# A new hand-written order for one segment of a memory recurrence, with filler copies, head sums and fold read at places of their own

## The chip, the cores and the metric

The kernel runs on one core of one Trainium2 chip. The metric is device time in microseconds of one execution; the profile is of one execution of the same program, taken by the hardware profiler, and its times are us from the first instruction.

## What is computed

Two attention blocks over the same 2048 tokens of width 576 are mixed by a gate. Block B is ordinary attention with 32 heads of width 18. Block A is a recurrence over 64 segments of 32 tokens: each segment sees 8 memory tokens and its own 32, and its first 8 outputs are the memory of the next.

```python
def _A_ref(x, mem0, Wq, Wk, Wv, Wo, seg_len):
    ...
    for s in range(n_seg):
        h = jnp.concatenate([mem, xs], axis=1)           # 8 + 32 tokens
        q, k, v = (einsum('btd,dhe->bhte', h, W) for W in (Wq, Wk, Wv))   # 32 heads of 128
        p = _softmax(where(mask, einsum('bhqe,bhke->bhqk', q, k) * scale, -1e9))
        o = einsum('bhte,hed->btd', einsum('bhqk,bhke->bhqe', p, v), Wo)
        mem = o[:, :M, :]
        outs.append(o[:, M:, :])
def _B_ref(x, wqkv, wo): ...                             # softmax attention, 32 heads of 18, no mask
return g * a + (1 - g) * b                               # g = sigmoid((x * gate_w).sum(-1))
```

## The kernel before, in words

**The stages.** A first part turns x, projects B's q, k and v and loads A's weights. Then come the 64 segments of A, one after the other; steps of B's attention are put between the steps of each segment. A last part finishes B, projects it out and mixes. The change lies in the segments and in two helpers that feed them.

**B's steps.** `b_steps` is a generator. Its first half, written `B` in the order, puts four score matmuls into `sb` (four PSUM banks, one buffer) and then the four value matmuls of the step before into `ob` (one bank, `values`, L239). Its second half, `E`, is one exp on ScalarE from `sb` to `etb` (L291). So the next `sb` has to wait for this exp, and the values come one step later. Every 16 steps a block of 512 queries is done: `ob` holds the sums and the weighted values of the 18-wide heads, and `divisions` (L178) puts six parts into the list `late`: two `turn_in` (a VectorE transpose that reads `ob`, L187), and then divide and turn_out twice. The next block can write `ob` only after both turn_in. `late_part` (L173) emits one part; `/` in the order calls it. Before the first value matmul of a new block all pending turn_in are emitted (L243).

**A segment.** The 32 kept tokens of `ht` (8 memory, 24 new; the last 8 tokens of each segment are projected ahead of time) go through these steps, with b = 0, 1 for two halves of the heads:

- Qb, Kb, Vb: projections into `pvv` (L672), 20 matmuls of 512 columns, four at a time on 32 columns of the array; cQb, cKb, cVb: copies to SBUF on VectorE (L684); vb: four DMAs on SP's queue that lay V out by heads in `v_sb` (L689).
- tqb, tkb: four transposes each into one PSUM tile `pt` (L699); pqb, pkb: the copies out of it (L707).
- Sb: scores into `psh` (L717); xb: exp on ScalarE (L728); nb: the causal minimum (L732); pb: sums by a matmul with `bsel` into `pss` (L739); lb, rb: log and exp(-log) on ScalarE (L743, L747); mb: the product with it (L750).
- wb0, wb1: the weighing by V into `pso` (L755); ob0, ob1: copies to `ot` (L767).
- a0b, a1b: output projection into `acc`, a0 384 and a1 192 columns wide (L575); h0, g0, h1, g1: `acc` split into an upper and a lower bf16 part `hl` (L586, L589).
- f0, f1: the fold, ten small matmuls by which the four partial sums are added and turned, into one PSUM tile `pw3` (L794); ht0, ht1: its memory columns go to the next segment's `ht` (L806; L808 to L810); og: its other columns go to `otsg` (L814).
- F0, F1, F2: fillers. Where nothing else is due, F1 and F2 each do one unit of `last_tokens` (L325): the projection of last tokens, 20 matmuls or 5, a copy of 512 columns on VectorE (L323) and a store. There are 72 units. Every fourth segment they do the outputs of four segments instead (`group_rows`, `group_span`, and `group_last` in the segment after).

**The order.** `ORDER` (L850) is written by hand, and inside the segments TensorE, ScalarE and VectorE issue exactly in it; SP and POOL don't stand under it. Three PSUM banks (tags b0 to b2) are left for a segment, and `BANKS` (L855) says which step takes which; the first writer of a bank waits until every reader of the tile before it is done. A matmul into a tile of which another part is being read waits for that read as well.

Of the kernel before, what the change touches and what calls it, by code (L numbers as in the profile page):

```python
# [16 lines left out]
def kernel(  # L17
# [15 lines left out]
    nc = tc.nc  # L33
# [183 lines left out]
    def b_steps():  # L217
# [21 lines left out]
        def values(g, kb, et4):  # L239
            nonlocal ob  # L240
            if kb == 0:

                while late and late[0][0].__name__ == "turn_in":  # L243
                    late_part()
                ob = ps_bo.tile([P, QC], FP32, name="ob")
            vc, o = vch[g, kb // KC], (kb % KC) * P
            last = None
            for j in range(4):
                mm = nc.tensor.matmul(  # L249
                    ob[32 * j:32 * j + 32, :],  # L250
                    lhsT=vc[:, o + 32 * j:o + 32 * j + 32],
                    rhs=et4[:, j, :],
                    start=(kb == 0),
                    stop=(kb == NKB - 1),
                    tile_position=(0, 32 * j),
                )
                if last is not None:
                    issue_behind(mm, last)
                last = mm
# [64 lines left out]

    def last_tokens(q, share, k=None):  # L325

        k = k or [None]
        store = nc.sync if share else nc.gpsimd
        xlb = fil.tile([P, NF + 2, P], BF16, name="xlb", bufs=1)
        nc.sync.dma_start(out=xlb[:, :, :].rearrange("p c t -> p (c t)"), in_=xld[q])  # L330
        for b in range(HD // 512):
            pv = bank(k[0], [P, 512], FP32, "pv")
            for c in range(NF + 1):
                rw, cc = w_slice(wv, c, b * 512, 512)
                nc.tensor.matmul(pv[:, :], lhsT=xlb[:, cc, :], rhs=rw, start=(c == 0), stop=(c == NF))
            vl = fil.tile([P, 512], BF16, name="vl")
            copy_out(vl[:, :], pv[:, :], share)
            store.dma_start(out=vld[q * P:(q + 1) * P, b * 512:(b + 1) * 512], in_=vl[:, :])
            yield
        for w, dstd in ((wq, qld), (wk, kld)):  # L340
            for b in range(H // 4):
                pv = bank(k[0], [P, 512], FP32, "pv")
                for h in range(4 * b, 4 * b + 4):
                    o = (h % 4) * P
                    for c in range(NF + 1):
# [2 lines left out]
                            pv[:, o:o + P], lhsT=lw, rhs=xlb[:, cc, :], start=(c == 0), stop=(c == NF)  # L348
                        )
                vl = fil.tile([P, 512], BF16, name="vl")  # L350
                copy_out(
                    vl[:, :].rearrange("p (s h t) -> p h s t", h=4, t=LO),
                    pv[:, :].rearrange("p (h s t) -> p h s t", s=SG, t=LO),
# [243 lines left out]
    def group_span(k, i):  # L597
        if i == 0:
            hlls[:] = [seg2.tile([P, 2, Dm], BF16, name="hll", bufs=1)]
        acc = bank(k, [P, 512], FP32, "accl")  # L600
        for b in range(2):
            out_project(acc, otl, b, *WSPAN[i])
        upper(acc, hlls[0], *WSPAN[i])
        lower(acc, hlls[0], *WSPAN[i])

    def group_last(k, s3):
        n = Dm // 3
        pl = bank(k, [P, n], FP32, "pl")
        for part in range(2):
            for i in range(3):  # L610
# [6 lines left out]
                    tile_position=(0, 32 * i),  # L617
                    skip_group_check=True,
                )
        rl = seg2.tile([P, n], BF16, name="rl", bufs=1)  # L620
        nc.vector.tensor_copy(out=rl[0:96, :], in_=pl[0:96, :])
        rows4 = a_dram[(s3 - 3) * seg:(s3 + 1) * seg, :].rearrange("(i q) d -> i q d", q=seg)
        for i in range(3):
            for m in range(4):
                nc.gpsimd.dma_start(
                    out=rows4[m, seg - LO:seg, i * n:(i + 1) * n],
                    in_=rl[32 * i + m * LO:32 * i + (m + 1) * LO, :],
                )

    def group_rows(k, s3):  # L630
        pto = bank(k, [P, Dm], BF16, "pto")
        for c in range(NF + 1):
            d0 = c * P if c < NF else T0
            nc.tensor.transpose(out=pto[:, d0:d0 + P], in_=otsg[:, c, :], identity=ident[:, :])
        oseg = seg2.tile([P, Dm], BF16, name="oseg", bufs=1)
        nc.vector.tensor_copy(out=oseg[:, :], in_=pto[:, :])
        rows4 = a_dram[(s3 - 3) * seg:(s3 + 1) * seg, :].rearrange("(i q) d -> i q d", q=seg)
        for i in range(4):
            nc.sync.dma_start(
                out=rows4[i, 0:seg - LO, :], in_=oseg[i * seg:(i + 1) * seg - LO, :]  # L640
            )

    def filler(s, i, k):

        if s >= 4 and (s % 4, i) == (0, 0):
            group_rows(k, s - 1)
        elif s >= 4 and (s % 4, i) in ((0, 1), (0, 2)):
            group_span(k, i - 1)
        elif s >= 4 and (s % 4, i) == (1, 0):
            group_last(k, s - 2)  # L650
        elif i > 0:
            fill_bank[0] = k
            next(later, None)

    def segment(s):

# [128 lines left out]
        def lower_part(i):  # L785
            lower(ps["a", i], sbt["hl"], *WSPAN[i])

        def fold(chunks, k):
            if "w" not in ps:
                ps["w"] = bank(k, [P, NF + 1, CT], FP32, "pw3")  # L790
            for c in chunks:
                d0 = c * P if c < NF else T0
                for part in range(2):
                    nc.tensor.matmul(  # L794
                        ps["w"][:, c, :],
                        lhsT=sbt["hl"][:, part, d0:d0 + P],
                        rhs=sel[:, :],
                        start=(part == 0),
                        stop=(part == 1),
                    )  # L800

        def memory(part):
            if s + 1 < n_seg:
                pw3 = ps["w"]
                if part == 0:
                    nc.vector.tensor_copy(out=hn[:, 0:3, 0:M], in_=pw3[:, 0:3, 0:M])  # L806
                else:
                    nc.vector.tensor_copy(out=hn[:, 3:NF, 0:M], in_=pw3[:, 3:NF, 0:M])  # L808
                    nc.vector.tensor_copy(out=hn[0:TL, NF, 0:M], in_=pw3[TL:P, NF, 0:M])
                    nc.vector.tensor_copy(out=hn[TL:P, NF + 1, 0:M], in_=pw3[TL:P, NF, 0:M])  # L810

        def rows():
            i4 = s % 4
            nc.vector.tensor_copy(out=otsg[:, :, i4 * seg:i4 * seg + CT - M], in_=ps["w"][:, :, M:CT])  # L814

        for x, w in (("Q", wq), ("K", wk), ("V", wv)):
            for b in range(2):
# [2 lines left out]
        for b in range(2):  # L820
# [18 lines left out]
        step("f0", fold, range(3), BANKS["pw"])  # L839
# [3 lines left out]
        step("og", rows)  # L843
# [15 lines left out]
    LAST_OT = 1  # L859

# [6 lines left out]
    for s in range(n_seg):  # L867
# [16 lines left out]
        for name in ORDER:  # L884
# [11 lines left out]
    group_rows(None, n_seg - 1)  # L896
    for i in range(2):
        group_span(None, i)
    group_last(None, n_seg - 1)
    actx.close()  # L900

    fin = ctx.enter_context(tc.tile_pool(name="fin", bufs=2, side="right"))
# [91 lines left out]
```

## Time and profile before

| | us |
|---|---|
| median of 3 runs (lowest to highest) | 1849.98 (1846.15 to 1853.02) |
| the profiled execution | 1850.31 |
| its span, first to last instruction | 1848.6 |
| TensorE busy | 1569.0 (85%) |
| ScalarE busy | 1150.3 (62%) |
| VectorE busy | 959.9 (52%) |
| mean granted TensorE clock | 0.922 of full speed |

TensorE's busy time counts matmuls that overlap once; its record of a matmul goes from its first read to a modelled end, so distances between starts say more than durations. "Idle before" an instruction is time in which its engine did nothing, with the instruction that ended it. The granted clock is 1.0 for 2.4 GHz and 0.5 for 1.2 GHz.

### The profile page before, as it was taken

The page shows a single profiled execution, that of the slowest core. Times are in us where ns is not written, and L with a number is a line of the kernel's source. Part 1 is how long each engine was busy: PE and PEld are TensorE (multiplying, and loading weights), DVE is VectorE, ACT ScalarE, POOL GpSimd, SP SyncE. Part 2 cuts the span into 40 slices and gives each one's busy share as a digit, 9 for nine tenths or more (in the row PEclk, how much of TensorE's full clock was granted, in tenths as well). Part 3 has the DMA queues.
Part 4 walks back from the last instruction along what each step waited for, and adds up shares of the span by engine and source line. Part 5 has one row for each costly group of instructions (what it writes and reads, how often), then busy time and mean ns, then how long its engine had stood idle before and what let it go on. Part 6 is the DMA issues. An engine that isn't in the chain of part 4 may idle for free.

```text
span 1848.6 us, 57724 instructions
## 1 busy us (share of the span) xinstructions
PE 1569.0 (85%) x25060; PEld 814.2 (44%) x25082; DVE 959.9 (52%) x2280; ACT 1150.3 (62%) x992; POOL 355.5 (19%) x694
## 2 busy tenths in 40 slices
PE   6487778888888888888888888988888898889886
PEld 3132344444444444444444444444444444444443
DVE  2022225555555565556555555555565555555553
ACT  2165666666666666656666666666666666766665
POOL 6110001121221213031313021312131202120110
PEclk9687889999999999999999999999998889988887
DMA  8755551111211111111212111111121111110005
GB/s 234 209 181 167 141 94 52 37 40 35 54 44 36 42 36 59 30 39 34 49 52 47 32 43 41 48 37 37 35 53 40 32 28 36 37 29 24 26 18 169
DMA packets 140521, 114.40 MB, mean 62 GB/s; under 512 B 75115, under 2 KB 128363, under 8 KB 138731
## 3 DMA queue, kind: packets, MB, share of 16 engines
q1 hardware_dynamic: 116612, 60.02, 12.3%
q0 software_dynamic: 18784, 44.40, 9.3%
q10 hardware_dynamic: 4871, 6.28, 1.1%
q8 instruction: 197, 3.23, 0.7%
q14 instruction: 57, 0.47, 0.1%
HBM read 57.72 MB, written 36.10 MB: 51 GB/s over the span
## 4 chain that ended last, share of the span: by engine, by line
PE 69%; DVE 14%; DMA 6%; ACT 6%; issue 3%; SPq 1%; POOL 0%; ACTq 0%; DVEq 0%; POOLq 0%
PE pvv L672 23%; PE acc L575 8%; PE sb L269 7%; PE ob L249 6%; PE pt L699 5%; PE pv L347 3%; PE psh L717 3%; PE pso L755 3%; ACT etb L291 3%; DVE hl L589 2%; DVE hl L586 2%; PE pq L435 2%; PE accl L575 2%; PE pss L739 2%; DMA vgd<-vt 2%
## 5 line engine op out<-in xcount | busy, mean ns | idle before, releaser
L291 ACT ACTIVATE etb<-sb 128x2048 bf16<-128x2048 f32 x512 | 960.6, 1876 | 414.9 <-PE sb L269 399.9
L684 DVE CAST tm<-pvv 128x512 bf16<-128x512 f32 x384 | 264.5, 689 | 205.9 <-PE pvv L672 205.8
L672 PEld LDWEIGHTS <-ht 128*32 128x32 bf16 x7680 | 192.0, 97 | 174.5 <-issue 4.2
L269 PE MATMUL sb<-qch,kch 32*128 32x512 bf16 x2048 | 218.0, 404 | 50.4 <-ACT etb L291 46.9
L249 PE MATMUL ob<-etb,vch 128*32 128x512 bf16 x2048 | 214.4, 408 | 9.9 <-DVE tq L187 9.1
L575 PE MATMUL acc<-wo,ot 128*32 128x384 bf16 (+1 forms) x4096 | 192.0, 347 | 0.0
L575 PEld LDWEIGHTS <-ot 128*32 128x32 bf16 x4096 | 115.5, 114 | 64.1 <-issue 34.2
L564 POOL COPY ht<-xg 128x144 bf16<-128x144 bf16 x64 | 19.6, 307 | 636.1 <-PE pvv L672 582.9
L672 PE MATMUL pvv<-wq_m,ht 128*32 128x512 bf16 x2048 | 136.5, 387 | 0.1
L672 PE MATMUL pvv<-wk_m,ht 128*32 128x512 bf16 x2048 | 134.0, 382 | 0.0
L672 PE MATMUL pvv<-wv_m,ht 128*32 128x512 bf16 x2048 | 133.4, 380 | 0.0
L699 PE MATMUL pt<-ident,tm 128*128 128x128 bf16 x1024 | 100.8, 221 | 33.0 <-DVE qt L707 33.0
L323 DVE CAST vl<-pv 128x512 bf16<-128x512 f32 x90 | 62.1, 691 | 123.9 <-PE pv L347 48.6
L767 DVE CAST ot<-pso 128x320 bf16<-128x320 f32 x256 | 118.8, 485 | 9.4 <-PE pso L755 4.2
L269 PEld LDWEIGHTS <-kch 32*128 32x128 bf16 x2048 | 56.8, 91 | 151.4 <-issue 132.1
L728 ACT ACTIVATE et<-psh 128x320 bf16<-128x320 f32 x128 | 56.0, 437 | 106.0 <-PE psh L717 105.9
L249 PEld LDWEIGHTS <-vch 128*32 128x32 bf16 x2048 | 53.9, 93 | 135.1 <-issue 131.3
L743 ACT ACTIVATE lt<-pss 128x320 f32<-128x320 f32 x128 | 55.7, 435 | 81.6 <-PE pss L739 81.6
L586 DVE CAST hl<-acc 128x384 bf16<-128x384 f32 (+1 forms) x128 | 58.0, 453 | 91.4 <-PE acc L575 90.8
L739 PE MATMUL pss<-et,bsel 128*128 128x320 bf16 x128 | 40.0, 312 | 74.5 <-DVE ot L767 74.5
L699 PEld LDWEIGHTS <-tm 128*128 128x128 bf16 x1024 | 60.1, 97 | 97.0 <-issue 57.9
L755 PE MATMUL pso<-et,v_sb 64*128 64x40 bf16 x2048 | 81.1, 183 | 22.8 <-DVE et L750 22.7
(131 smaller groups left out, 1956.3 us busy)
## 6 DMA issues: line engine op xcount, KB each, us to landing
v_sb<-tm SPq DMA_DIRECT2D x512, 32.0 KB
wo<-in_A_Wo_dram SPq DMA_DIRECT2D x4, 1152.0 KB
wv_m<-in_A_Wv_dram POOLq DMA_DIRECT2D x4, 1024.0 KB, 7.7
qch<-qtd POOLq DMA_DIRECT2D x32, 128.0 KB, 2.5
kch<-ktd POOLq DMA_DIRECT2D x32, 128.0 KB, 2.7
vgd<-vt SPq DMA_DIRECT2D x32, 128.0 KB
vch<-vgd POOLq DMA_DIRECT2D x32, 128.0 KB, 2.5
wq_m<-in_A_Wq_dram POOLq DMA_DIRECT2D x4, 1024.0 KB, 7.1
```

The lines of the kernel that those rows point to most:

```text
L249: mm = nc.tensor.matmul(ob[32 * j:32 * j + 32, :], lhsT=vc[:, o + 32 * j:o + 32 * j + 32], rhs=et4[:, j, :], start=(kb == 0), stop=(kb == ...
L269: mm = nc.tensor.matmul(sb[:, j, :], lhsT=kc[32 * j:32 * j + 32, o:o + P], rhs=qch[gq][32 * j:32 * j + 32, :], start=True, stop=True, tile ...
L291: nc.scalar.activation(out=before[:, :, :], in_=sb[:, :, :], func=ACT.Exp, scale=scale_b)
L323: nc.vector.tensor_copy(out=out, in_=in_)
L575: nc.tensor.matmul(acc[32 * j:32 * j + 32, 0:d1 - d0], lhsT=o[:, h, 0:CT], rhs=wo[:, h, d0:d1], start=(b == 0 and i == 0), stop=(b == 1 an ...
L586: nc.vector.tensor_copy(out=hl[:, 0, d0:d1], in_=acc[:, 0:d1 - d0])
L672: nc.tensor.matmul(pv[32 * j:32 * j + 32, :], lhsT=ht[:, cc, :], rhs=rw, start=(c == 0), stop=(c == NF), tile_position=(0, 32 * j),)
L684: nc.vector.tensor_copy(out=sbt[x][:, :], in_=ps[x][:, :])
L699: nc.tensor.transpose(out=pt[:, which, :, :, :].rearrange("p j (u i) t -> p j u i t", i=4)[:, :, :, i, :], in_=sbt[x][:, i * Dh:(i + 1) * Dh],
L739: nc.tensor.matmul(ps["p", b][:, 0:W8], lhsT=bsel[:, :], rhs=et[:, b, :], start=True, stop=True)
L755: nc.tensor.matmul(pso[:, i * L:(i + 1) * L], lhsT=v_sb[64 * jj:64 * jj + 64, b * 1024 + i * Dh:b * 1024 + (i + 1) * Dh], rhs=et[64 * jj:6 ...
L767: nc.vector.tensor_copy(out=ot[:, j * HG:(j + 1) * HG, :].rearrange("p h t -> p (h t)"), in_=ps["o", b, jj][:, 0:W8],)
```

## The change

`ORDER` and `BANKS` are written anew. In the new order the copy of a filler is a step of its own (cF0, cF1, cF2): `filler` and the group functions do their matmuls and hand back a function for the rest, and `last_tokens` yields a second time, ahead of each copy. A new mark `:` stands behind each E and calls `free_sums`, which emits all pending turn_in. The fold writes two PSUM tiles, `pw0` (chunks 0 to 2) and `pw1` (chunks 3 and 4), in two banks; the copy og is split into og and oh, one from each. The numbers of matmuls, exps, copies and DMAs are the same otherwise; each segment has seven B, seven E and three `/` as before.

```diff
+    def free_sums():
+        while late and late[0][0].__name__ == "turn_in":
+            late_part()
...
             if kb == 0:
-                while late and late[0][0].__name__ == "turn_in":
-                    late_part()
+                free_sums()
                 ob = ps_bo.tile([P, QC], FP32, name="ob")
...
             vl = fil.tile([P, 512], BF16, name="vl")
+            yield
             copy_out(vl[:, :], pv[:, :], share)
...
-    for _ in last_tokens(0, 4):
-        b_advance(1)
+    for i, _ in enumerate(last_tokens(0, 4)):
+        b_advance(i % 2)
...
     def filler(s, i, k):
         if s >= 4 and (s % 4, i) == (0, 0):
-            group_rows(k, s - 1)
+            return group_rows(k, s - 1)
...
+        fill_bank[0] = k
+        next(later, None)
+        return lambda: next(later, None)
...
-        def fold(chunks, k):
-            if "w" not in ps:
-                ps["w"] = bank(k, [P, NF + 1, CT], FP32, "pw3")
+        def fold(part, k):
+            chunks = (range(3), range(3, NF + 1))[part]
+            ps["w", part] = bank(k, [P, len(chunks), CT], FP32, f"pw{part}")
...
-        step("f1", fold, range(3, NF + 1), BANKS["pw"])
+        step("f1", fold, 1, BANKS["pv"])
...
+        def fill(i):
+            rest[i] = filler(s, i, BANKS[f"F{i}"])
+
         for i in range(3):
-            step(f"F{i}", filler, s, i, BANKS[f"F{i}"])
+            step(f"F{i}", fill, i)
+            step(f"cF{i}", lambda i: rest[i](), i)
...
     ORDER = """
-        Q0 B K0 V0 cQ0 tq0 cK0 E B pq0 E tk0 Q1 cV0 pk0 S0 B K1 v0 x0 cQ1 n0 p0 / V1 cK1 E / / B l0
-        r0 cV1 tq1 pq1 tk1 pk1 E v1 F1 S1 B m0 x1 n1 w00 F2 o00 p1 E l1 F0 r1 w01 B E m1 o01 w10 w11
-        a00 o10 o11 a01 a10 h0 a11 g0 h1 B E f0 g1 ht0 f1 ht1 og
+        Q0 cQ0 K0 B E : cK0 / K1 tq0 tk0 pq0 V0 cK1 B E : pk0 Q1 S0 cV0 cQ1 x0 tk1 n0 B E : tq1 pk1
+        V1 pq1 p0 cV1 l0 r0 / S1 m0 v0 B F1 w00 x1 n1 o00 F2 cF1 p1 w01 E : v1 B l1 cF2 o01 r1 m1 E
+        : F0 a00 w10 cF0 w11 B E : o10 o11 a01 a10 a11 B / E : h0 g0 h1 g1 f0 ht0 f1 ht1 og oh
     """.split()
     BANKS = dict(
-        Q0=0, K0=2, V0=1, t0=0, Q1=2, S0=0, K1=1, p0=0, V1=2, t1=1, w00=0, w01=2, S1=1, p1=0, A0=2,
-        F0=1, F2=2, F1=2, w10=1, w11=0, A1=0, pw=1,
+        Q0=1, K0=2, V0=1, t0=2, Q1=2, S0=0, K1=0, p0=2, V1=0, t1=1, w00=2, w01=0, S1=1, p1=2, A0=0,
+        F0=2, F2=1, F1=0, w10=1, w11=2, A1=1, pw=2, pv=0,
     )
...
             elif name == "/":
                 late_part()
+            elif name == ":":
+                free_sums()
```

In this text B1 to B7 and E1 to E7 are the seven B and E of a segment in their order, and p1, w10 and so on are the steps by the names above.

## Rows read from the trace of the kernel before

**Rows 1.** The page: span; busy us, share of span and instructions by engine.

```profile
span 1848.6 us, 57724 instructions
PE 1569.0 (85%) x25060; PEld 814.2 (44%) x25082; DVE 959.9 (52%) x2280; ACT 1150.3 (62%) x992; POOL 355.5 (19%) x694
```

**Rows 2.** Line L809: duration ns min/median/max, first and last start us.

```profile
L809 DVE CAST ht<-pw x63: 167/168/171, 293.6 to 1769.9; 64x8 bf16<-64x8 f32 x63
```

**Rows 3.** TensorE's waits, 294 to 1790: us in total, times, longest us.

```profile
PE pss L739 <- DVE ot L767: 73.3, 63, 1.3
PE pt L699 <- DVE qt L707: 32.5, 63, 0.5
PE pw L794 <- DVE ht L806: 22.9, 62, 0.4
PE pso L755 <- DVE et L750: 22.2, 60, 0.5
```

**Rows 4.** Timeline, TensorE: start, duration, instructions, idle before and releaser.

```profile
915.50 3.42 PE L575 MATMUL acc<-wo,ot 128*32 128x384 bf16 x64
...
920.44 1.05 PE L672 MATMUL pvv<-wq_m,ht 128*32 128x512 bf16 x16
...
923.26 1.04 PE L672 MATMUL pvv<-wv_m,ht 128*32 128x512 bf16 x16
...
924.45 0.40 PE L699 MATMUL pt<-ident,tm 128*128 128x128 bf16 x4
...
931.30 0.40 PE L699 MATMUL pt<-ident,tm 128*128 128x128 bf16 x4
...
932.21 0.38 PE L699 MATMUL pt<-ident,tm 128*128 128x128 bf16 x4 [0.52 <-DVE qt L707]
...
937.67 0.30 PE L739 MATMUL pss<-et,bsel 128*128 128x320 bf16 x1 [1.27 <-DVE ot L767]
...
939.35 0.48 PE L755 MATMUL pso<-et,v_sb 64*128 64x40 bf16 x16 [0.43 <-DVE et L750]
...
939.76 2.41 PE L575 MATMUL acc<-wo,ot 128*32 128x384 bf16 x64
...
942.10 0.39 PE L269 MATMUL sb<-qch,kch 32*128 32x512 bf16 x4
...
943.68 0.83 PE L672 MATMUL pvv<-wq_m,ht 128*32 128x512 bf16 x12
```

**Rows 5.** Timeline of the same segment, ScalarE: r1 and E7.

```profile
938.47 0.47 ACT L747 ACTIVATE rq<-lt 128x320 bf16<-128x320 f32 x1
...
942.55 1.88 ACT L291 ACTIVATE etb<-sb 128x2048 bf16<-128x2048 f32 x1 [1.84 <-PE sb L269]
```

**Rows 6.** Timeline of the same segment, VectorE: h0 and h1.

```profile
941.55 0.56 DVE L586 CAST hl<-acc 128x384 bf16<-128x384 f32 x1 [0.92 <-PE acc L575]
...
942.62 0.35 DVE L586 CAST hl<-acc 128x192 bf16<-128x192 f32 x1
```

**Rows 7.** Line L187 (turn_in), the whole span; below, who waited for it.

```profile
L187 DVE STREAM_TRANSPOSE tq<-ob x64: 407/439/450, 139.2 to 1836.2; 128x256 f32<-128x256 f32 x64
...
  PE ob L249: 9.1, 12
```

**Rows 8.** Stretches: busy us by engine, granted clock, DMA share, GB/s.

```profile
294.00:1790.00 1496.00, 1327.86 (x23078) 695.04 (x23081) 868.42 (x2080) 975.04 (x819) 291.49 (x570) 0.95 0.15 39
915.50:918.00 2.50, 2.50 (x35) 1.25 (x36) 0.85 (x2) 0.85 (x1) 0.40 (x1) 0.50 0.65 130
939.80:942.10 2.30, 2.30 (x66) 1.48 (x64) 1.38 (x3) 0.91 (x1) 0.40 (x1) 1.00 0.24 53
```

**Rows 9.** Timeline, same segment: v0 on SP, cV1, then SP's stores.

```profile
925.93 3.35 SPq L689 DMA_DIRECT2D v_sb<-tm  x4
...
930.99 0.65 DVE L684 CAST tm<-pvv 128x512 bf16<-128x512 f32 x1
...
931.09 1.35 SPq L209 DMA_DIRECT2D otd<-stage  x4
```

More of the change, by code (lines that the diff above doesn't have):

```diff
@@ L602, in group_span, with rest @@
             out_project(acc, otl, b, *WSPAN[i])
-        upper(acc, hlls[0], *WSPAN[i])
-        lower(acc, hlls[0], *WSPAN[i])
+        def rest():
+            upper(acc, hlls[0], *WSPAN[i])
+            lower(acc, hlls[0], *WSPAN[i])
+        return rest
     def group_last(k, s3):
@@ L619, in group_last, with rest @@
                 )
[L620 to L628, printed above, removed]
+        def rest():
+            rl = seg2.tile([P, n], BF16, name="rl", bufs=1)
+            nc.vector.tensor_copy(out=rl[0:96, :], in_=pl[0:96, :])
+            rows4 = a_dram[(s3 - 3) * seg:(s3 + 1) * seg, :].rearrange("(i q) d -> i q d", q=seg)
+            for i in range(3):
+                for m in range(4):
+                    nc.gpsimd.dma_start(
+                        out=rows4[m, seg - LO:seg, i * n:(i + 1) * n],
+                        in_=rl[32 * i + m * LO:32 * i + (m + 1) * LO, :],
+                    )
+        return rest
     def group_rows(k, s3):
@@ L634, in group_rows, with rest @@
             nc.tensor.transpose(out=pto[:, d0:d0 + P], in_=otsg[:, c, :], identity=ident[:, :])
[L635 to L641, printed above, removed]
+        def rest():
+            oseg = seg2.tile([P, Dm], BF16, name="oseg", bufs=1)
+            nc.vector.tensor_copy(out=oseg[:, :], in_=pto[:, :])
+            rows4 = a_dram[(s3 - 3) * seg:(s3 + 1) * seg, :].rearrange("(i q) d -> i q d", q=seg)
+            for i in range(4):
+                nc.sync.dma_start(
+                    out=rows4[i, 0:seg - LO, :], in_=oseg[i * seg:(i + 1) * seg - LO, :]
+                )
+        return rest
     def filler(s, i, k):
         if s >= 4 and (s % 4, i) == (0, 0):
-            group_rows(k, s - 1)
[L647 to L653, printed above, removed]
+            return group_rows(k, s - 1)
+        if s >= 4 and (s % 4, i) in ((0, 1), (0, 2)):
+            return group_span(k, i - 1)
+        if s >= 4 and (s % 4, i) == (1, 0):
+            return group_last(k, s - 2)
+        if i == 0:
+            return lambda: None
+        fill_bank[0] = k
+        next(later, None)
+        return lambda: next(later, None)
     def segment(s):
@@ L786, in lower_part @@
             lower(ps["a", i], sbt["hl"], *WSPAN[i])
-        def fold(chunks, k):
-            if "w" not in ps:
-                ps["w"] = bank(k, [P, NF + 1, CT], FP32, "pw3")
+        def fold(part, k):
+            chunks = (range(3), range(3, NF + 1))[part]
+            ps["w", part] = bank(k, [P, len(chunks), CT], FP32, f"pw{part}")
             for c in chunks:
                 d0 = c * P if c < NF else T0
-                for part in range(2):
+                for r in range(2):
                     nc.tensor.matmul(
-                        ps["w"][:, c, :],
-                        lhsT=sbt["hl"][:, part, d0:d0 + P],
+                        ps["w", part][:, c - chunks[0], :],
+                        lhsT=sbt["hl"][:, r, d0:d0 + P],
                         rhs=sel[:, :],
-                        start=(part == 0),
-                        stop=(part == 1),
+                        start=(r == 0),
+                        stop=(r == 1),
                     )
@@ L803, in memory, with rows @@
             if s + 1 < n_seg:
-                pw3 = ps["w"]
+                pw = ps["w", part]
                 if part == 0:
-                    nc.vector.tensor_copy(out=hn[:, 0:3, 0:M], in_=pw3[:, 0:3, 0:M])
+                    nc.vector.tensor_copy(out=hn[:, 0:3, 0:M], in_=pw[:, :, 0:M])
                 else:
[L808 to L814, printed above, removed]
+                    nc.vector.tensor_copy(out=hn[:, 3, 0:M], in_=pw[:, 0, 0:M])
+                    nc.vector.tensor_copy(out=hn[0:TL, NF, 0:M], in_=pw[TL:P, 1, 0:M])
+                    nc.vector.tensor_copy(out=hn[TL:P, NF + 1, 0:M], in_=pw[TL:P, 1, 0:M])
+        def rows(part):
+            c0, c1 = ((0, 3), (3, NF + 1))[part]
+            i = s % 4 * seg
+            nc.vector.tensor_copy(out=otsg[:, c0:c1, i:i + CT - M], in_=ps["w", part][:, :, M:CT])
         for x, w in (("Q", wq), ("K", wk), ("V", wv)):
@@ L895 @@
     ordered.close()
-    group_rows(None, n_seg - 1)
+    group_rows(None, n_seg - 1)()
     for i in range(2):
-        group_span(None, i)
-    group_last(None, n_seg - 1)
+        group_span(None, i)()
+    group_last(None, n_seg - 1)()
     actx.close()
```

7 lines of the change are left out of this document (5 added, 2 removed).

## The prediction

> **What bounds the kernel now.** I read the page first, for the busy engine. TensorE is busy for 85% of the span, ScalarE for 62%, VectorE for 52% [rows 1]: the first is close to the bound, but none is full. Then I asked where one turn of the recurrence ends: the last copies of the new memory (L809) come 63 times, from 293.6 to 1769.9 us [rows 2], so the 64 segments take 1476.3 / 62 = 23.81 us each and some 1500 of the 1849 us. Only there does the change act: the loop over `last_tokens(0, 4)` now yields twice per unit and calls `b_advance(0)` and `b_advance(1)` in turn, which is the old sequence, and the tail calls the same work. Then the waits of TensorE: four kinds come once in nearly every segment, the sums `pss` behind `ot` 73.3 us, a transpose behind `qt` 32.5, the fold behind `ht` 22.9, the weighing `pso` behind `et` 22.2 [rows 3]. Last, one undisturbed segment in order of time, from the Q0 at 920.44 to the next at 943.68, 23.24 us [rows 4]; its steps give the prices below.
>
> So a segment is bound by the hand-written TensorE order, with holes where a PSUM bank isn't free in time. Each hole, from start to start: tk1 begins 0.91 after tq1 though four transposes last 0.22, **0.69**. p1 follows F2; it sits idle 1.27 us for `ot`, and a p1 right behind transposes or F2 needs no change of array shape (0.11), so with the sequencer's share **1.46**. w10 waits **0.50** for m1. The four `acc` steps take 2.34 where 2 x 0.65 + 2 x 0.33 = 1.96 would do, **0.38**. f1 waits **0.4** for ht0. Sum 3.43; own work of a segment 23.24 - 3.43 = 19.8 [rows 3, 4].
>
> **The change part by part.** *Removed holes.* p1: in the old order DVE copies F2's filler ahead of o00, and p1 takes o00's bank; in the new one o00 stands before both filler copies, and F2 (1.1 us of matmuls) runs on TensorE meanwhile. tk1: tq0 and tk0, later tk1 and tq1, now come with no copy of their own bank between them. w10: its m1 needs l1 and r1 (r1 takes 0.47 us on ScalarE [rows 5], l1 a little less), and now B5 and a00 lie between. a01: o10 and o11 now have B6 over them. f1 has its own bank (0) and no longer waits for ht0, only for g1. All five go to about nothing; what is late next is read from a walk.
>
> *The walk*, at the full clock. The steps are distances from start to start in the stretch of which rows 4 show the ends and the holes (a projection: 923.26 to 924.45): a projection 1.19 (1.08 ahead of another), sb 0.32, ob 0.33 (0.23 ahead of a projection), scores 0.51, sums 0.24, a weighing 0.30, a filler 1.21 or 1.10. Q0 at 0, K0, B1 at 2.27, K1, tq0, tk0, V0, B2 at 5.75, Q1, S0, tk1, B3 at 8.33, tq1, V1, p0, S1, B4 at 11.25, F1, w00 at 13.11, F2, p1, w01, B5 at 15.04. An exp starts 0.45 after its sb and takes 1.88, and the next sb follows 0.05 behind it [rows 4, 5]. E1 to E4 end at 4.6, 8.1, 10.7 and 13.95 (E4 stands behind l0, r0 and x1), always before the next B. From here **ScalarE is what is late**: l1 starts 14.84, r1 ends 15.78, so E5 runs 15.71 to 17.59 and B6 can't begin before 17.64. TensorE has done a00 (which waits until 15.91 for o01, same bank) and w10, w11 by 17.07: a new hole of 0.57. Behind B6 come a01, a10, a11 to 19.62; E6 ends 19.97: B7 at 20.02, a hole of 0.40. Meanwhile DVE does h0 from 19.05 (0.56 each for h0 and g0, 0.35 each for h1 and g1 [rows 6]) to g1's end at 20.87; f0 20.67, f1 20.93, ht0 to 21.14, next Q0 at 21.2. Per undisturbed token segment **-2.05 us**.
>
> *Sum over the segments.* 72 units of `last_tokens` go in pairs: 36 segments with tokens, 36 x 2.05 = 73.8. 15 segments (s = 4, 8, ...) carry group_span; their 1.28 and 0.66 us of matmuls replace the tokens', and their DVE copies are longer (0.56 + 0.56, 0.36 + 0.36), so I take 1.8, an estimate: 27. 13 late segments have no filler; there o00 isn't covered and B5 waits for E4: the same walk gives p1 at 13.15, B5 at 14.0, B6 at 16.38, B7 at 18.76, next Q0 about 20. The old order also had smaller holes there; I take 1.2: 15.6. Together -116. Bounds: 1.0 to 2.2 per segment, -64 to -141.
>
> *The sums of the 18-wide heads.* The two turn_ins (0.44 each [rows 7]) now stand right behind the E of the B in which the product ends; before, they stood just ahead of the next B. That saves TensorE's wait at ob, 9.1 us in all over 12 cases [rows 7], but DVE is in order, and what is behind waits for this B's product (sb + 0.77) plus 0.85. There are 28 divisions, four at each of the seven Bs, and the walk prices each place: at B7, h0 slips from 19.05 to 21.64, about +2.4; at B6, o10 slips from 17.1 to 19.26 and a01 with it, +1.7 after the hole at B7 is used up; at B2, pk0 and so Q1 (its bank), +1.5; at B1, cK0 and tq0, +0.6; the others 0 to 0.3. Mean 0.94, x 28 = +26; less the 9 that goes, **+16** taken. This part by itself I expect to cost. Bounds -9 to +40.
>
> *The fold in two tiles* adds one DVE copy (og and oh for one of 0.28 us), some 0.15 us behind ht1, where DVE waits for Q0 anyway: nothing; if not covered, 64 x 0.15 = 10.
>
> *The clock.* The granted clock is 0.95 over the stage; with the levels 2.4 and 1.2 GHz a tenth of 1496 us ran at the lower one [rows 8], and at most half of that, 75 us, is lost. In the segment before my example the `acc` steps ran at 0.50, behind p1's and w10's holes, and took 3.42 us; in the example at 1.00 and 2.41 us [rows 4, 8]. The holes shrink from 3.4 to about 1.4 us per segment (21.2 - 19.8), 1.0 of it at B6 and B7. I take **-10**, between +35 (below) and -40.
>
> *V's way through SBUF* (v0, v1): each is four DMAs from SP's queue. Four took 3.35 us to issue when nothing else was there, and SP also carries the stores of `stage`, 1.35 us, which had just delayed v1 [rows 9]. Before, cV1 ended at 931.64 and w10 began at 939.35 [rows 4, 9], 7.7 us; in the walk cV1 ends at 11.3 and w10 begins at 16.7, 5.4 us. No row shows the landing itself; w10 needs only the first two, so I take zero cost and keep the other end as a rival. otl, ht and the loads on POOL keep their places relative to what they wait for.
>
> Sum: -116 + 16 - 10 = -110 against the profiled execution's own 1850.3 us (span 1848.6 and 1.7 around it; the median is 1850.0): **1740 us**.
>
> **The rivals.** *The clock takes it back.* The holes at B6 and B7 stand 1 to 3 us behind w00, p1 and w01, which are short matmuls, much as the old holes at p1 and w10 did. If the level falls there in each segment, all four `acc` steps lie in it: 3.42 us instead of 2.41 [rows 4, 8], 1.0 x 64 = 64 lost instead of the some 30 that my sum leaves: 1740 + 35 = 1775, up to 1790 if f and Q0 run slow too. For it: the old holes, which did bring it, were also made of short waits beside short matmuls; against it: fewer and shorter holes. The Trainium skill, "TensorE: Matmul & The Clock Gate", section "A second HAM failure mode: psum-queue depth-cycling", says that a kernel whose matmul groups cycle through PSUM banks idles for moments between groups and that the clock then swings between its levels. The trace agrees so far as 0.50 and 1.00 follow each other in neighbouring segments; by that page the new order, which cycles the same three banks, would go on swinging. Chance 0.13. *The clock never falls*: about 30 us more, 1710: 0.08.
>
> *V comes late, and the kernel is slower.* If SP holds v1 behind stage stores or behind loads that wait for POOL, w10 and w11 wait, and with them the longest chain of the segment (a01, h0, fold). Each us that V lands beyond 5.4 us after cV1's end costs a us in each segment, once the hole at B6 (0.5) is used up. The gain of 110 is 1.7 per segment, so from 5.4 + 0.5 + 1.7 = 7.6 us on the change loses: at 8 us it would be 1740 + 64 x (8 - 5.9) = 1874. Against it: the issue of four took 3.35 us alone and 4.8 behind stage stores, so I give it 0.05; and 0.06 that it is late in some segments only, 1770 to 1835.
>
> *The removed holes were not the bound*, and the exp chain or the DVE order stops the gain at half: 64 x 0.9 = 58, 1790. Against it the walk, in which E1 to E4 each end 0.2 to 1.2 us before the B that waits for them. 0.06. The forecast itself: 0.62.
>
> **How the numbers follow.** The forecast's own range, from the bounds of the segment term, the divisions and the clock together, is 1715 to 1765. To hold 8 in 10 it must reach into the low clock and the half gain, and down to the clock that never falls: 1710 to 1790. Faster by over 0.5% (which is about what a measurement of this kernel can tell from no change): all but the V that is late in each segment and a rest, 0.92; within 0.5%: 0.03; slower: 0.05.
>
> **What would show it.** L809's copies should come every 21 to 23 us instead of 23.8. Among TensorE's waits, pss behind `ot` and pw behind `ht` should be gone, and sb behind `etb`, now rare, should stand first with about 1 us per segment. ScalarE's share should rise above 65%. Wrong would be: a wait of pso on a DMA (V late), a granted clock below 0.93 in the stage, or h0 or o10 behind `tq` costing more than 40 us in all. A time above 1790 would mean that the walk missed a bound on one of the five removed holes.

## The result, and the profile after

The changed kernel takes 1716.5 us (median, 1705.6 to 1720.9) against 1850.3 of the kernel before beside it on the chip: a ratio of 0.927, interval 0.922 to 0.932. Measured again in the first experiment it is 1717.1 against 1846.2, 0.930, interval 0.927 to 0.933. So the change saves 129 to 134 us. The forecast was 1740 us, 110 less than before.

Four views of the changed kernel answer the rows of before. First the page (busy us, share of the span, instructions by engine), for [rows 1]:

```profile
span 1713.7 us, 57820 instructions
PE 1511.4 (88%) x25082; PEld 792.7 (46%) x25082; DVE 962.7 (56%) x2344; ACT 1148.1 (67%) x992; POOL 351.8 (21%) x694
```

The last copy of the new memory is now L830 (duration ns min/median/max, first and last start), for [rows 2]:

```profile
L830 DVE CAST ht<-pw x63: 167/168/170, 286.6 to 1634.0; 64x8 bf16<-64x8 f32 x63
```

From first to last that is 1347.4 us, or 21.73 per segment, where it was 1476.3 and 23.81: 128.9 us less between the same two marks. The first mark also comes 7 us earlier in this profile. That is not the change's doing, or not all of it: the changed kernel profiled again has it at 290.2, and a kernel shown below, whose code ahead of the segments is that of the kernel before, at 286.3. What follows the last copy is as long as it was (79.7 and 78.7 us).

TensorE's waits in the stage, 293 to 1660 (us in total, times, longest), for [rows 3]:

```profile
PE sb L272 <- ACT etb L294: 34.1, 76, 0.8
PE pso L775 <- DVE hll L595: 9.7, 14, 0.8
PE pss L759 <- DVE ot L787: 8.7, 14, 0.7
PE acc L581 <- DVE ot L787: 6.8, 7, 1.3
PE pso L775 <- DVE et L770: 6.2, 13, 0.6
...
PE pso L775 <- DMA v_sb<-tm: 4.4, 6, 1.4
```

The four waits that came in nearly every segment, 151 us together [rows 3], are gone or left in 13 or 14 segments only; what stands first now is TensorE waiting for ScalarE's exp. The same view of VectorE has a new row, VectorE waiting for the last product of a block so as to turn it:

```profile
DVE tq L192 <- PE ob L252: 27.6, 20, 2.9
```

The stage as one stretch (busy us by engine, granted clock, DMA share, GB/s), for [rows 8]:

```profile
293.00:1660.00 1367.00, 1269.96 (x23090) 674.20 (x23091) 872.55 (x2146) 973.07 (x819) 286.93 (x568) 0.99 0.17 42
```

The granted clock is 0.99 where it was 0.95. With the levels 2.4 and 1.2 GHz that is some 2% of 1367 us at the lower one, 27 us, instead of 10% of 1496, 150 us. Last, the steps of TensorE in one segment from its Q0 to the next (start, duration, instructions, idle before and releaser), for [rows 4]:

```profile
809.74 1.05 PE L692 MATMUL pvv<-wq_m,ht 128*32 128x512 bf16 x16
...
825.39 0.34 PE L621 MATMUL pl<-hll,sel 128*32 128x192 bf16 x6
825.65 0.83 PE L581 MATMUL acc<-wo,ot 128*32 128x384 bf16 x16
826.41 0.49 PE L775 MATMUL pso<-et,v_sb 64*128 64x40 bf16 x16
827.46 0.40 PE L272 MATMUL sb<-qch,kch 32*128 32x512 bf16 x4 [0.55 <-ACT etb L294]
827.79 0.40 PE L252 MATMUL ob<-etb,vch 128*32 128x512 bf16 x4
828.01 1.48 PE L581 MATMUL acc<-wo,ot 128*32 128x384 bf16 x48
829.83 0.40 PE L272 MATMUL sb<-qch,kch 32*128 32x512 bf16 x4 [0.34 <-ACT etb L294]
830.16 0.40 PE L252 MATMUL ob<-etb,vch 128*32 128x512 bf16 x4
830.49 0.50 PE L815 MATMUL pw<-sel,hl 128*128 128x32 bf16 x10
831.08 1.05 PE L692 MATMUL pvv<-wq_m,ht 128*32 128x512 bf16 x16
```

It takes 21.34 us, of which 0.26 (825.39 to 825.65) is the group's last part, which the walk of the prediction left out: 21.1 beside the 21.2 foretold. The only idle of a third of a microsecond or more is at B6 (827.46) and B7 (829.83), both behind the exp.

### The profile page after: what moved, and what is told of

It reads as the page before. It is cut to its first block, busy times and chain, and to the rows that moved or that the text cites. A ratio compares the mean times of both kernels' runs of the same rounds, so it can differ in the third digit from the quotient of the medians.

```text
span 1713.7 us, 57820 instructions
## 1 busy us (share of the span) xinstructions
PE 1511.4 (88%) x25082; PEld 792.7 (46%) x25082; DVE 962.7 (56%) x2344; ACT 1148.1 (67%) x992; POOL 351.8 (21%) x694
## 4 chain that ended last, share of the span: by engine, by line
PE 64%; ACT 16%; DVE 8%; DMA 7%; issue 3%; SPq 2%; POOL 0%; ACTq 0%; DVEq 0%; POOLq 0%
PE pvv L692 25%; ACT etb L294 13%; PE sb L272 9%; PE ob L252 6%; PE pt L719 5%; PE pv L352 3%; PE psh L737 3%; PE acc L581 2%; PE pv L339 2%; PE pq L441 2%; DMA vgd<-vt 2%; PE pso L775 2%; DVE hl L595 2%; DVE hl L592 1%; ACT rq L767 1%
## 5 line engine op out<-in xcount | busy, mean ns | idle before, releaser
L252 PE MATMUL ob<-etb,vch 128*32 128x512 bf16 x2048 | 210.9, 401 | 0.4 <-ACT etb L294 0.4
L581 PE MATMUL acc<-wo,ot 128*32 128x384 bf16 (+1 forms) x4096 | 159.2, 292 | 9.0 <-DVE ot L787 6.8
L272 PEld LDWEIGHTS <-kch 32*128 32x128 bf16 x2048 | 66.8, 91 | 188.6 <-issue 166.9
L581 PEld LDWEIGHTS <-ot 128*32 128x32 bf16 x4096 | 103.9, 98 | 52.9 <-issue 14.5
L727 DVE COPY qt<-pt 128x512 bf16<-128x512 bf16 x128 | 53.7, 419 | 90.1 <-PE pt L719 89.8
L637 POOL DMA_DIRECT2D a_dram<-rl x192 | 96.4, 554 | 24.8 <-DVE rl L633 20.4
L775 PEld LDWEIGHTS <-v_sb 64*128 64x128 bf16 x2048 | 61.6, 93 | 70.2 <-issue 57.2
L719 PE MATMUL pt<-ident,tm 128*128 128x128 bf16 x1024 | 90.5, 221 | 1.6 <-DVE tm L704 1.6
```

Source lines behind the costliest of these rows:

```text
L252: mm = nc.tensor.matmul(ob[32 * j:32 * j + 32, :], lhsT=vc[:, o + 32 * j:o + 32 * j + 32], rhs=et4[:, j, :], start=(kb == 0), stop=(kb == ...
L272: mm = nc.tensor.matmul(sb[:, j, :], lhsT=kc[32 * j:32 * j + 32, o:o + P], rhs=qch[gq][32 * j:32 * j + 32, :], start=True, stop=True, tile ...
L581: nc.tensor.matmul(acc[32 * j:32 * j + 32, 0:d1 - d0], lhsT=o[:, h, 0:CT], rhs=wo[:, h, d0:d1], start=(b == 0 and i == 0), stop=(b == 1 an ...
L637: nc.gpsimd.dma_start(out=rows4[m, seg - LO:seg, i * n:(i + 1) * n], in_=rl[32 * i + m * LO:32 * i + (m + 1) * LO, :],)
L719: nc.tensor.transpose(out=pt[:, which, :, :, :].rearrange("p j (u i) t -> p j u i t", i=4)[:, :, :, i, :], in_=sbt[x][:, i * Dh:(i + 1) * Dh],
L775: nc.tensor.matmul(pso[:, i * L:(i + 1) * L], lhsT=v_sb[64 * jj:64 * jj + 64, b * 1024 + i * Dh:b * 1024 + (i + 1) * Dh], rhs=et[64 * jj:6 ...
```

## The experiments

Theory: the gain is holes taken out of TensorE's order, above all p1's behind the filler's copy, with ScalarE's exp late next; the turn_ins' early place costs; the clock is worth little. Rivals: the order of the products alone does it; the early place is a gain; the clock is a large part of it.

### One part undone at a time

The changed kernel again, for the three beside it:

> The changed kernel itself, so that the three that follow have it beside them on the same chip: 1716 us, ratio to the kernel before 0.927, with its last copies of the memory every 21.7 us.

Measured: 1717.1 us, ratio 0.930.

**The filler copies put back** right behind their products, and o00 behind F2's copy; all else of the changed kernel stays:

```diff
-  B F1 w00 x1 n1 o00 F2 cF1 p1 w01 E : v1 B l1 cF2 o01 r1 m1 E : F0 a00 w10 cF0
+  B F1 cF1 w00 x1 n1 F2 cF2 o00 p1 w01 E : v1 B l1 o01 r1 m1 E : F0 cF0 a00 w10
```

> The changed kernel's order of TensorE, but every filler copy goes straight behind its own matmuls again, and o00 behind F2's copy, as it stood before; banks, fold and turn_ins are the changed kernel's. Theory: p1 waits for o00 again, 1.3 to 1.5 us in the 51 segments with a filler, 60 to 90 us in all: 1780 to 1805, with pss behind ot first among TensorE's waits at over 60 us. Rival: with the new order of the products the exp chain bounds the segment anyway, and the copies' place is worth less than 20 us: under 1737.

Measured: 1785.9 us, ratio 0.968 (0.965 to 0.971), 68.8 us slower than the changed kernel. Its waits of TensorE in the stage, and its stage:

```profile
PE pss L759 <- DVE ot L787: 67.1, 59, 1.5
PE sb L272 <- ACT etb L294: 47.9, 101, 0.8
```

```profile
294.00:1725.00 1431.00, 1274.04 (x22994) 671.59 (x23001) 877.45 (x2137) 969.67 (x817) 288.00 (x568) 0.98 0.16 40
```

p1's wait for o00 is back nearly as it was [rows 3], and its 67 us are about the whole difference. The theory holds for this part. No run puts the holes at tk1, w10 and a01 back one by one; that they are gone is read from the waits above. But mark the clock: 0.98 with the same hole that stood in a stage at 0.95 before.

**The fold in one tile** again, so that f1 waits for ht0:

```diff
-            ps["w", part] = bank(k, [P, len(chunks), CT], FP32, f"pw{part}")
+            if part == 0:
+                ps["w"] = bank(k, [P, NF + 1, CT], FP32, "pw3")
```

> The changed kernel with the fold in one PSUM tile again (f1's two chunks in the tile that ht0 reads). Theory: f1 waits for ht0 again and with it the next segment's Q0, 0.2 to 0.4 us in each of 64 segments: 11 to 26 us slower than the changed kernel, 1727 to 1742, and pw behind ht is back among TensorE's waits. Rival: f1 is held by g1 at least as long, so the second tile does nothing: 1716.

Measured: 1729.2 us, ratio 0.937 (0.934 to 0.940), 12.1 slower than the changed kernel, 0.19 per segment. f1's wait for ht0 is among TensorE's waits in the stage again:

```profile
PE pw L816 <- DVE ht L827: 18.4, 62, 0.5
```

That is 0.30 each time. The second tile is worth half of the 0.4 per segment that the prediction counted.

**The turn_ins where they were**, every ':' taken out:

```diff
-  Q0 cQ0 K0 B E : cK0 / K1 ... V0 cK1 B E : pk0 ... a11 B / E : h0 g0 ...
+  Q0 cQ0 K0 B E cK0 / K1 ... V0 cK1 B E pk0 ... a11 B / E h0 g0 ...
```

> The changed kernel with every ':' taken out of ORDER, so that the two turn_ins of the 18-wide heads' sums stand where they stood before the change, ahead of the next block's first value product (or at a '/'). Theory, the prediction's step: VectorE waits for the block's product with o10, h0 or pk0 queued behind it, which costs 16 us net; then this kernel is 10 to 20 us faster than the changed one, about 1700, and the 2.4 us longer segments (a division at B7) shrink. Rival: the early place pays for itself, because TensorE otherwise waits for tq at ob (9 us over 12 cases before); then this kernel is at 1716 or up to 10 us slower, and the wait of TensorE's ob for tq is back.

Measured: 1708.3 us, ratio 0.926 (0.923 to 0.929), 8.8 faster than the changed kernel: the early place costs, but the shift is below the 10 to 20 expected. VectorE's wait for the product didn't go as a whole; the row of the stage, and one of the places on its timeline:

```profile
DVE tq L192 <- PE ob L252: 13.1, 8, 2.9
```

```profile
939.51 0.45 DVE L192 STREAM_TRANSPOSE tq<-ob 128x256 f32<-128x256 f32 x1 [2.90 <-PE ob L252]
939.88 0.52 DVE L592 CAST hl<-acc 128x384 bf16<-128x384 f32 x1
```

The '/' that stands ahead of h0 takes the first turn_in itself when a product ends at B7, and h0 stands behind 2.90 us of waiting as in the changed kernel. So that place was not undone. A later run moved this '/' too:

```diff
-  ... a11 B / E h0 g0 h1 g1 f0 ht0 f1 ht1 og oh
+  ... a11 B E h0 g0 h1 g1 f0 ht0 f1 ht1 og oh /
```

> As the kernel without ':' (1708.3 us, 8.8 under the changed kernel), and with the last '/' moved from ahead of h0 to the end of the segment. Without the ':' that '/' still puts the first turn_in ahead of h0 when a product ends at B7: VectorE waits 2.90 us there and that segment takes 23.4 us instead of 21.35, in 4 of 28 divisions. Theory, the prediction's prices by place: these 4 x 2.05 = 8 us go too, 1700, so that the whole early place costs 16 to 17 us against the changed kernel. Rival: what h0 saves is lost again at TensorE's ob in the next block, which then waits for both turn_ins: 1706 to 1712.

Measured: 1695.5 us, ratio 0.918 (0.915 to 0.921), 12.8 less than with the '/' there, and 21.6 less than the changed kernel. The 8 expected for B7 are exceeded; the moved '/' also moves other parts of `late` (divide, turn_out), and their share isn't parted from it. VectorE's waits in the stage:

```profile
DVE tq L192 <- PE ob L252: 2.2, 4, 0.6
```

The rival, that TensorE's ob takes the wait over, falls: ob waits for tq 8.0 us in 8 cases in both of these kernels. The early place costs some 20 us. The marks of this kernel are used further down:

```profile
L830 DVE CAST ht<-pw x63: 167/169/170, 285.8 to 1613.9; 64x8 bf16<-64x8 f32 x63
```

### What the clock is worth, and which hole moves it

Two kernels of the old order that touch p1's hole, and a third that touches w10's. First two words exchanged in the old ORDER, so that VectorE copies o00 ahead of the filler; TensorE's order is the same:

```diff
-  ... m0 x1 n1 w00 F2 o00 p1 E l1 ...
+  ... m0 x1 n1 w00 o00 F2 p1 E l1 ...
```

> The kernel before with two words of ORDER exchanged, 'o00 F2' for 'F2 o00', so that VectorE copies o00 ahead of F2's filler; TensorE's order, the banks, the fold and the turn_ins stay. Theory: p1's hole, worth 68.8 us when put back into the changed kernel (1785.9 - 1717.1), is a cause of its own, and taking it out of the old order gives 50 to 70 us, or up to 95 if the lower clock also goes with it: 1751 to 1796, and pss behind ot leaves the first place of TensorE's waits. Rival: in the old order the next weighing (w01) and its copies are late at once, and less than 35 us comes: above 1811.

Measured: 1750.8 us, ratio 0.947 (0.944 to 0.950): 98.5 us less, more than the theory's upper end, from two words. Its marks and its stage:

```profile
L809 DVE CAST ht<-pw x63: 167/169/171, 286.3 to 1668.9; 64x8 bf16<-64x8 f32 x63
```

```profile
294.00:1689.00 1395.00, 1277.81 (x22954) 677.93 (x22957) 864.79 (x2069) 973.15 (x815) 290.29 (x567) 0.98 0.17 41
```

Then the old order with the hole left as it is, and work put into it: four products that nothing reads, ahead of p1.

```diff
+        def extra():
+            px = bank(1, [P, 512], FP32, "px")
+            for i in range(4):
+                nc.tensor.matmul(px[:, :], lhsT=bsel[:, :], rhs=wq[0][:, 0, i * 512:(i + 1) * 512], start=True, stop=True)
-  ... w00 F2 o00 p1 E l1 ...
+  ... w00 F2 o00 D p1 E l1 ...
```

> The kernel before with four products of 512 columns that nothing reads (0.85 us of TensorE at the higher level) put ahead of p1 in each segment, into the PSUM bank that is free there; nothing is left out. They lie in p1's hole of 1.27 us. It prices the clock: the stage's granted clock is 0.95 before and 0.99 after. Theory: the hole at p1 is what lets the clock fall, so that more work makes the kernel faster: the granted clock of the stage rises to 0.98 or more, and the time falls by 20 to 50 us, to 1796 to 1826. Rival one: the clock falls for other holes (w10's, or the short products around it), stays at 0.95, and the time is within 10 us of 1846. Rival two: the products don't fit the hole and cost up to 64 x 0.85 = 54 us: up to 1900.

Measured: 1805.8 us, ratio 0.977 (0.974 to 0.979). With 256 products more and nothing less to do the kernel is 43.5 us faster:

```profile
L814 DVE CAST ht<-pw x63: 167/169/171, 288.3 to 1725.0; 64x8 bf16<-64x8 f32 x63
```

```profile
294.00:1745.00 1451.00, 1327.22 (x23198) 692.64 (x23253) 863.66 (x2074) 970.32 (x818) 290.91 (x567) 1.00 0.16 40
```

The stage goes from 1476.3 to 1436.7 us (first to last mark) and the granted clock from 0.95 to 1.00. An undisturbed segment is as long as it was, 23.23 to 23.33 from copy to copy beside 23.25; the segments of 24.3 us and more, 22 of 62 before, are those that become rare, 4 of 62. So the products fill time in which TensorE stood still, and what is gained is the clock: 43.5 us (39.6 of them between the marks), four times the prediction's -10.

The gain of 98.5 of the two words is clock and hole together. An undisturbed segment falls to 22.03 us from 23.25, and 1.2 in each of the 51 segments with a filler would be some 61 us for the hole; the other 37 or so are then clock, since the stage is at 0.98 here and not at 1.00. This split is an estimate.

Last, the old order with w10's hole filled in the same way, by two products (bank 0, behind o01):

```diff
-  ... B E m1 o01 w10 w11 ...
+  ... B E m1 o01 D w10 w11 ...
```

> The kernel before with two products of 512 columns that nothing reads (0.43 us at the higher level) put into the hole ahead of w10 (0.50 us) instead of p1's; p1's hole stays. Putting four into p1's hole took 43 us off with segments otherwise the same, while p1's hole in the new order leaves the clock at 0.99. Theory: the level falls for the idle time of the whole stretch from p1 to w11 together, so that filling w10's hole helps as well: granted clock of the stage 0.97 to 0.99 and 15 to 45 us less, 1803 to 1833. Rival: p1's hole alone brings it in the old order: the clock stays at 0.95 to 0.96 and the time within 10 us of 1848. Second rival: the products don't fit and cost up to 64 x 0.43 = 28 us.

Measured: 1848.0 us, ratio 1.001 (0.999 to 1.004). Its stage, and the place on TensorE's timeline:

```profile
294.00:1790.00 1496.00, 1331.02 (x23124) 693.48 (x23189) 867.48 (x2080) 974.76 (x819) 290.50 (x568) 0.96 0.16 39
```

```profile
837.06 0.40 PE L249 MATMUL ob<-etb,vch 128*32 128x512 bf16 x4
837.39 0.39 PE L744 MATMUL px<-wq_m,bsel 128*128 128x512 bf16 x1
837.93 0.49 PE L760 MATMUL pso<-et,v_sb 64*128 64x40 bf16 x16
```

The products lie between ob and w10 (one of the two is missing from the record). The time is that of the kernel before, and so is the stage, 1476.3 us from mark to mark:

```profile
L814 DVE CAST ht<-pw x63: 167/168/170, 290.9 to 1767.2; 64x8 bf16<-64x8 f32 x63
```

By its number the rival holds, and my theory's 15 to 45 us don't come. But two things cancel behind that number. The products don't quite fit: at the full clock an undisturbed segment takes 23.30 us beside 23.25, and every fourth segment, with the outputs of four, 23.99 beside 23.75, some 9 us in 62 segments. And the clock did move: over the whole execution it is 0.932 to 0.945 in the ten runs of this kernel, and 0.918 to 0.929 in the thirteen of the kernel before beside it. Twice the missing share of the clock is the share of time at the lower level; by the medians that is some 45 us less at that level, a third of the 137 or so that the products at p1 took away (0.962 beside 0.926). So w10's hole has a part in the clock as well, the smaller one, and what the clock gives back here, the products take.

The two runs differ in the amount of work too, 0.43 us and 0.85, so that the place alone decides isn't shown. Why p1's hole leaves 0.98 in the new order (the 0.99 of the expectation is the stretch from 300 to 1640) is open as well. There F1 stands right ahead of w00, and B5 and a00 lie between w01 and w10; no run moved these alone.

### Whether ScalarE is the bound

The same cut in both kernels: the exp of the 18-wide heads over three of its four blocks of columns.

```diff
-                nc.scalar.activation(out=before[:, :, :], in_=sb[:, :, :], func=ACT.Exp, scale=scale_b)
+                nc.scalar.activation(out=before[:, 0:3, :], in_=sb[:, 0:3, :], func=ACT.Exp, scale=scale_b)
-                    rhs=et4[:, j, :],
+                    rhs=et4[:, min(j, 2), :],
```

> The changed kernel with the exp of the 18-wide heads over three of its four blocks of 512 columns (about 1.45 us instead of 1.88; the value products of the fourth head of each group read the third's, and its sums are wrong by that); TensorE's work is the same. Theory, the prediction's walk: in the new order ScalarE is what is late, at B6 and B7, 0.97 us per undisturbed segment; with the shorter exp both holes go, the last copies of the memory come every 20.7 to 21.1 us instead of 21.7 (40 to 65 us off the stage), and sb behind etb falls from 79 to below 25 us. Rival: TensorE's own order is the bound in the new kernel too, and the waits for etb only fill time that it would lose elsewhere: the copies stay within 0.3 us of 21.7.

> The same cut (the exp of the 18-wide heads over three of four blocks, the fourth head reading the third's) in the kernel before, to be read beside the cut in the changed one. Theory: before the change the segments were bound by holes that DVE and the banks made, not by ScalarE; the last copies of the memory go from every 23.8 us to no less than 23.5 (under 20 us off the stage), what the whole kernel gains lies ahead of the first of them. Rival: the exp chain was already the bound, and the stage gains as much as that of the changed kernel, 40 us or more.

Measured: the changed kernel with the cut 1683.9 us, ratio 0.911 (0.907 to 0.915); the kernel before with it 1832.3, ratio 0.991 (0.988 to 0.995). The marks of the stage, first of the changed kernel with the cut, then of the one before with it:

```profile
L830 DVE CAST ht<-pw x63: 167/169/170, 274.8 to 1601.6; 64x8 bf16<-64x8 f32 x63
```

```profile
L809 DVE CAST ht<-pw x63: 167/169/169, 275.3 to 1749.5; 64x8 bf16<-64x8 f32 x63
```

Before, the stage goes from 1476.3 to 1474.2 us: nothing hangs on ScalarE there. After, from 1347.4 to 1326.8, 20.6 us: something does, but not the 40 to 65 expected. TensorE's waits in the stage of the changed kernel with the cut, and the end of one segment, show why:

```profile
PE pw L815 <- DVE hl L595: 13.6, 63, 0.4
...
PE sb L272 <- ACT etb L294: 1.9, 9, 0.2
```

```profile
830.58 1.67 PE L581 MATMUL acc<-wo,ot 128*32 128x384 bf16 x48
832.18 0.40 PE L272 MATMUL sb<-qch,kch 32*128 32x512 bf16 x4
832.50 0.40 PE L252 MATMUL ob<-etb,vch 128*32 128x512 bf16 x4
832.84 0.45 PE L815 MATMUL pw<-sel,hl 128*128 128x32 bf16 x7
833.49 0.24 PE L815 MATMUL pw<-sel,hl 128*128 128x32 bf16 x3 [0.20 <-DVE hl L595]
```

The waits for the exp go from 34.1 us to 1.9, but f1 now waits for g1, in every segment: B6 and B7 come earlier and h0, which needs a01, does not come earlier by as much. VectorE's four copies of hl are late next. My expectation also read the 79 us of the whole span, of which 45 lie outside the segments.

### Two other orders

They keep the changed kernel's code and take another ORDER and other BANKS, with no ':'.

```diff
+        K0 B Q0 V0 E cK0 tk0 cQ0 tq0 pq0 B pk0 K1 Q1 / E cV0 S0 B cK1 x0 cQ1 n0 E tq1 v0 p0 tk1 l0
+        r0 / pk1 V1 pq1 S1 x1 B cV1 m0 n1 E w00 o00 p1 v1 F1 w01 B l1 r1 cF1 m1 o01 F0 F2 cF0 E w11
+        w10 B o10 o11 a00 a01 a10 a11 E B cF2 h0 g0 h1 E g1 f0 ht0 / f1 ht1 oh og
+        Q0=2, K0=1, V0=0, t0=1, Q1=1, S0=0, K1=2, p0=2, V1=0, t1=1, w00=0, w01=0, S1=1, p1=2, A0=0,
+        F0=1, F2=2, F1=1, w10=0, w11=1, A1=1, pw=2, pv=0,
```

> The changed kernel with another ORDER and other BANKS, and no ':'. F2 stands behind w01 and m1's work, so that two filler products lie under the last exp-bound stretch ahead of w10 and w11, K0 begins the segment, and the last two blocks of the 18-wide heads stand further apart from each other. Theory: what is left in the changed kernel are holes at B6, B7, f1 and the turn_ins' places, about 1.4 us per segment over TensorE's own work of 19.8; an order that spaces the blocks to the exp's 1.88 us gets an undisturbed segment to 20.2 to 20.6 us and the whole to 1640 to 1665. Rival: VectorE's copies h0 to g1 ahead of the fold are late as soon as the exp is not, and the whole stays above 1690.

Measured: 1695.3 us, ratio 0.918 (0.915 to 0.920). The theory's 1640 to 1665 are missed, and the time is the rival's, above 1690, but not for the rival's reason: the copies of hl stand only third. Its waits of TensorE in the stage:

```profile
PE pso L775 <- DMA v_sb<-tm: 32.5, 42, 2.7
PE pso L775 <- DVE et L770: 12.1, 62, 0.5
PE pw L815 <- DVE hl L595: 11.5, 57, 0.2
```

w11 and w10 stand closer behind V's copy here, and V's way through SBUF is the first wait: the prediction's rival, in another kernel. One place on its timeline, V's copy, its DMAs on SP and the product that waits:

```profile
851.67 0.69 DVE L704 CAST tm<-pvv 128x512 bf16<-128x512 f32 x1 [0.45 <-PE pvv L692]
...
853.13 2.41 SPq L709 DMA_DIRECT2D v_sb<-tm  x4
...
857.42 0.56 PE L775 MATMUL pso<-et,v_sb 64*128 64x40 bf16 x16 [0.51 <-DMA v_sb<-tm]
```

From the end of the copy (852.36) to the product it is 5.06 us.

```diff
+        K0 B Q0 cK0 K1 E cQ0 tq0 tk0 pk0 B V0 cK1 pq0 Q1 E S0 cV0 B cQ1 v0 x0 tk1 E n0 / tq1 pq1 p0
+        V1 pk1 S1 l0 / r0 B cV1 x1 E m0 w00 n1 o00 F1 p1 l1 F2 cF1 w01 B r1 F0 cF2 E o01 v1 cF0 a00
+        m1 w10 o10 w11 o11 B / E a01 a10 h0 a11 g0 h1 B f0 g1 f1 ht0 ht1 og oh E
+        Q0=2, K0=0, V0=0, t0=2, Q1=1, S0=2, K1=1, p0=1, V1=0, t1=2, w00=1, w01=0, S1=2, p1=2, A0=1,
+        F0=2, F2=1, F1=0, w10=2, w11=0, A1=2, pw=1, pv=2,
```

> The changed kernel with a second ORDER and BANKS without ':', in which F1 and p1 are taken together, a00 stands ahead of m1 and w10, and the seventh exp is left to run under the next segment's first projections. Theory: same as for the first of the two orders, somewhat more wait left at the blocks: 1650 to 1680. Rival: the exps then come too late for the next segment's first blocks, and the whole is above 1690.

Measured: 1676.0 us, ratio 0.908 (0.905 to 0.910), as the theory has it and 41 us under the changed kernel, in which the early turn_ins alone cost some 20. Its waits of TensorE in the stage:

```profile
PE sb L272 <- ACT etb L294: 22.4, 86, 0.8
PE pso L775 <- DMA v_sb<-tm: 14.2, 17, 1.9
PE ob L252 <- DVE tq L192: 11.7, 15, 1.2
```

The exp's wait is a third shorter than in the changed kernel, and the others come in 17 segments at most.

## Why the prediction was right, and where its terms were not

The time lies in the range, 23 us under the forecast, and the holes as the main gain are shown. That it fell inside owes something to luck: 1716.5 is 1.5 us above the lower end of the forecast's own range, 1715, and the fastest of its four runs, 1705.6, is under 1710. The terms one by one:

- *Holes, -116.* The walk holds: 21.1 us for the segment where it said 21.2, holes of 0.55 and 0.34 at B6 and B7 where it said 0.57 and 0.40. The 0.05 us from an exp's end to the next sb, which rows 4 and 5 don't show, is there in the changed kernel (827.41 to 827.46). The term as a whole can be read from two kernels that both run the stage at 0.99 or 1.00: the new order without the early turn_ins, 1695.5 us (1328.1 between the marks), and the old one with the products at p1, 1805.8 (1436.7), 110 us apart, the fold included. Putting p1's hole back costs 68.8 us; the step's 1.46 per segment is 1.35 in an undisturbed one by that run (22.70 beside 21.35). f1's 0.4 was twice too much: the second tile is worth 0.19 per segment.
- *The turn_ins, +16 (26 less 9).* The sign was right against what the part is meant to do, and the price by place too: where the product ends at B7, VectorE waits 2.90 us ahead of h0. Undone at all places it is worth 21.6 us; the 9 of ob's wait that I credited is 8.0.
- *The fold's extra copy, 0.* Hidden, or at least smaller than the 12 us that the second tile gives.
- *The clock, -10.* This is the step that failed. I took the smaller holes to matter in proportion and put the price near the middle of bounds from +35 to -40. The extra products measure -43.5 in the old order, outside these bounds, with the stage's granted clock at 1.00; the changed kernel's 0.99 says that nearly all of it came there too. Which of the new order's differences brought it isn't known, since the clock stays at 0.98 with p1's hole put back. With -43.5 for the clock and +21.6 for the turn_ins the sum is 1850.3 - 116 + 21.6 - 43.5 = 1712, 4 under the 1716.5 measured.
- *V's way, 0.* Right, by little. Waits of pso on that DMA, which I had named as a sign of being wrong, are 4.4 us in 6 cases, and the first of the two other orders shows the way to be 5.06 us long in one place, beside the walk's 5.4 from copy to product. A closer order pays for it, 32.5 us there.

Of the rivals, the clock that takes it back in each segment is out: holes at B6 and B7 stand there as foretold, and the clock is at 0.99. The Trainium skill, "TensorE: Matmul & The Clock Gate", section "A second HAM failure mode: psum-queue depth-cycling", has the clock swing for short idle between groups that cycle through PSUM banks. The new order cycles the same three banks and swings little (0.99), so the trace agrees only for the old order (0.95), and there the products in one hole took most of it away. The clock that never falls, 0.08 at 1710, was nearest to the time and got too small a chance. Half the gain is out as well: the exp chain is what is late next, and VectorE's copies of hl behind it, but what they hold back is the 0.9 us at B6 and B7 that the walk had.

Of the signs foretold, the waits for `ot` and `ht` going, ScalarE's 67% and 21.7 us between the copies came. The wait of sb for the exp is first, but 0.5 us per segment instead of 1, since it comes 76 times and not at both blocks of each.

## What to carry to other kernels

In a hand-written order over few PSUM banks, read for each product which copy frees its bank and what stands ahead of that copy on its engine: two words exchanged gave 98.5 of 1849 us, most of what the whole rewrite gave. Where the granted clock is below 1 in a stage, price it by an experiment, harmless products put into one hole at a time: here one hole gave 43.5 us back and another, with half the work, nothing on balance. A copy that is taken early on an in-order engine costs its wait to all that stands behind it, so try each part of a bundled change alone: one of these three lost 20 us.

## What the runs showed of the chip that I had not expected

Adding 0.85 us of TensorE work per segment made the kernel 43.5 us faster, with the granted clock of the stage up from 0.95 to 1.00, while 0.43 us of work in the next hole brought the clock to 0.96 and left the time where it was (1848.0 us). A hole of about the same length at the same product in another order left the clock at 0.98. And in one place four DMAs of 32 KB within SBUF, issued in 2.41 us, made the product behind them start 5.06 us after the copy that they read had ended.
